# Attention and a gated FFN woven into one instruction stream: the first batch's attention set alone, whole 512-token FFN tiles, even FFN shares, the range count in two parts

## The chip, the cores and the metric

The kernel runs on one core of a Trainium2 chip. The core has a matrix engine (TensorE, PE in the rows), a vector engine (VectorE, DVE), a scalar engine (ScalarE, ACT), a general engine (GpSimd, POOL) and a queue processor (SyncE, SP); 16 DMA engines move data between the device memory (HBM) and the on-chip memory (SBUF), and matmul results go to PSUM, which has eight banks. The metric is the device time of one execution in microseconds; lower is better.

## The reference

Causal attention over 8 batches of 8 heads with 576 positions of 64 numbers, with 16 beacon keys and values ahead of each sequence that every position sees; its output, laid out as 4608 tokens of 512 numbers, goes through a gated feed-forward layer (FFN) of width 1536.

```python
k_all = np.concatenate([beacon_k, k], axis=2)
v_all = np.concatenate([beacon_v, v], axis=2)
scores = scale * np.matmul(q, k_all.transpose(0, 1, 3, 2))
...
scores = np.where(causal, -1000000000.0, scores)
a = np.exp(scores - max)
a /= a.sum(-1, keepdims=True) + 1e-09
x = np.matmul(a, v_all)          # then as 4608 x 512 tokens
...
gate = np.maximum(x @ w_gate, 0.0)
return (gate * (x @ w_val)) @ w_out
```

## The kernel before

The whole program is one list of instructions per engine, written out by a planner in Python; each engine takes its list in order and waits where a buffer or an operand is not ready. Attention for a batch is cut into seven **steps**, and the FFN is cut into nine tiles of 512 tokens. A table `plan` says for each step which batch's attention it holds and how many microseconds of FFN work (the quota) may be put beside it.

**Attention of one step.** A step holds two units. `Unit.qk` writes scores into one of two double-bank PSUM buffers (`s`, L322), `Unit.exp` takes them through the exponential on ScalarE into `e` (L330) and masks the diagonal parts on GpSimd (`affine_select`, L338). When the last unit of a chunk (240, 256 or 80 positions of four heads) has gone, the next step computes `Chunk.av`: the products with the values into `ab` and the row sums into `os` (L364), both in PSUM with one buffer each. `invert` takes the reciprocal of the row sums on VectorE (`r`, L372), `scale` multiplies it into `xT`, the FFN's input (L377), and `report` sends one copy of `r` per head to `rsum` through SP (L384). For batches 0 and 1 the units run chunk by chunk through both groups of four heads (`UNITS_BY_CHUNK`), for the others group by group.

**FFN of one tile.** Twelve `up` groups and four `down` groups. An `up` group is four matmuls into `g` with the gate's weights (L399), a Relu on ScalarE (L402), four matmuls into `u` with the other weights (L405), and the product on VectorE into `hT` (L407). `g` and `u` take turns in the two buffers of the PSUM pool `f_ps`, so the next `g` waits for the Relu and the next `u` for the product. A `down` group is twelve matmuls (L412), a copy on ScalarE (L415) and a store by SP (L417). Tiles 0 and 1 are cut in two pieces each, (0, 240), (240, 512), (512, 816), (816, 1024), so that a piece can start as soon as a chunk of the batch is there; the others are whole. Each step hands groups from `queue` to the lists as long as its credit lasts.

**Loading.** Batches 0 and 1 load k and q in halves (`load_half`, L256, tile `wide`), cast them (`hwide`, L263) and turn them with transposing matmuls through `f_ps` (L274); their 64 last rows go through `turn_rows` (L291, the tails). v is loaded by rows (L226, `raw`) and cast (L241). Batches 2 to 7 are fetched one batch ahead: loads on SP, casts on GpSimd into the pool `half`, and DMA transposes on SP (L250). The weights come in by casting DMAs that GpSimd issues (L298, L303).

**The end.** After step 58 the rest of the queue is emitted in a plain loop. At its fifth group `count_in_range` checks on VectorE that all row sums lie in a range (three operations on `rsum`, a 1-column matmul, L433, and a cast) and loads the count into a register of every engine; after the loop a branch on it skips or runs a general path, which the inputs here don't need.

Of the kernel before, what the change touches and what calls it, by code (L numbers as in the profile page):

```python
# [153 lines left out]
def kernel(  # L154
# [12 lines left out]
    nc = tc.nc  # L167
# [30 lines left out]
    stage = main.enter_context(tc.tile_pool(name="stage", bufs=8))  # L198
    half = main.enter_context(tc.tile_pool(name="half", bufs=6))
    psb = main.enter_context(tc.tile_pool(name="psb", bufs=10))  # L200
    nrm = main.enter_context(tc.tile_pool(name="nrm", bufs=2))
    fsb = main.enter_context(tc.tile_pool(name="fsb", bufs=2))
# [5 lines left out]
    class Batch:  # L208
# [50 lines left out]
        def cast_half(self, x, i, cast):  # L259
            raw = self.raw.pop((x, i, "half")).rearrange("p (h r d) -> p r h d", r=2, d=D)  # L260
            h = self.h[x, i, "half"] = wide.tile([P, 2, d_model], BF16, name="hwide", bufs=2)
            for r in range(2):
                cast(h[:, r].rearrange("p (h d) -> p h d", d=D), raw[:, r])  # L263
# [79 lines left out]
    class Chunk:  # L343
# [6 lines left out]
        def av(self):  # L350
            self.ab = o_ps.tile([P, 2, 256], FP32, name="ab")
            self.os = o_ps.tile([P, 256], FP32, name="os")
            cq0, _, segs = CHUNKS[self.ci]
            order = sorted(segs, key=lambda x: x[0])
            for i, (kt, q0, n, _, _) in enumerate(order):
                e = self.batch.e.pop((self.g, self.ci, kt))
                kr = min(P, Stot - kt * P)
                for part in range(3):
                    for hh in range(4):
                        rows = slice(hh * C, (hh + 1) * C)  # L360
                        c0 = (4 * self.g + hh) * D + part * C
                        w = ones[:kr, :] if part == 2 else self.batch.v[:kr, kt, c0:c0 + C]
                        o = self.os[rows] if part == 2 else self.ab[rows, part]
                        nc.tensor.matmul(  # L364
                            o[:, q0 - cq0:q0 - cq0 + n], w, e[:kr, 2 * (hh % 2) + hh // 2],
                            start=(i == 0 and part != 1), stop=(i == self.last),
                            skip_group_check=True)
# [55 lines left out]

    def count_in_range():
        rows = B * H
        ge = const.tile([rows, S], FP32, name="ge")
        nc.vector.tensor_scalar(out=ge, in0=rsum, scalar1=1e-10, scalar2=None, op0=ALU.is_ge)
        nc.vector.scalar_tensor_tensor(out=ge, in0=rsum, scalar=1e10, in1=ge,
                                       op0=ALU.is_le, op1=ALU.mult)
        ok = const.tile([rows, 1], BF16, name="ok")  # L430
        nc.vector.tensor_reduce(ok, ge, op=ALU.min, axis=AX.X)
        cnt_ps = o_ps.tile([1, 1], FP32, name="os")
        nc.tensor.matmul(cnt_ps, ok, ones[:rows, :1], start=True, stop=True)  # L433
        cnt = const.tile([1, 1], mybir.dt.int32, name="cnt")
        nc.vector.tensor_copy(cnt, cnt_ps)
        return nc.values_load(cnt, min_val=0, max_val=rows,
                              skip_runtime_bounds_check_because="a count of rows")

# [5 lines left out]

    plan = ([(0, i, 4.5 if i > 4 else 0.0) for i in range(STEPS)]
            + [(None, 0, 4.5)] * ALONE
            + [(1, i, 4.0) for i in range(STEPS)]
            + [(b, i, 4.5) for b in range(2, B) for i in range(STEPS)]
            + [(None, 0, 4.5)])

    with tc.manual_schedule():
# [10 lines left out]
        def load_first(x):  # L462
            x.beacon = x.load_rows(beacon_k[x.b])
            x.load_half("k", 0)
            x.load_half("q", 0)
            x.load("v", 0)
            x.load("v", 1)

        def load_rest(x):
            x.load_half("k", 1)  # L470
            x.load_half("q", 1)
            x.load("v", 2)
            x.load("v", 3)
            x.tail_k = x.load_rows(k[x.b, :, 512:])
            x.tail_q = x.load_rows(q[x.b, :, 512:])
            x.load("v", 4)
# [7 lines left out]
        first.cast_half("q", 0, act)  # L484
        first.turn_half("q", 0, (act, dve))
        first.cast("v", 0, pool)
        first.cast("v", 1, pool)

# [4 lines left out]
        def turn_two(x, i, cast):  # L493
            for n in "kq":
                x.cast_half(n, i, cast)
                x.turn_half(n, i, (dve, act))
# [7 lines left out]
        at(0, lambda: turn_two(first, 1, dve))  # L504
        at(0, lambda: load_both(384, 768))
        at(1, lambda: None)
        at(1, lambda: load_both(768, 1536))
        at(2, lambda: first.cast("v", 2, pool))
        at(2, lambda: first.cast("v", 3, pool))
        at(3, lambda: turn_tails(first))  # L510
        at(4, lambda: batches.update({1: Batch(1)}))
# [17 lines left out]
        at(second - 1, lambda: turn_two(batches[1], 1, pool))  # L529
        at(second - 1, lambda: batches[1].cast("v", 1, pool))  # L530
        at(second + 1, lambda: batches[1].cast("v", 2, pool))
        at(second + 1, lambda: batches[1].cast("v", 3, pool))
        at(second + 2, lambda: turn_tails(batches[1]))
        at(second + 3, lambda: batches[1].cast("v", 4, pool))
        at(second + 3, wide_ctx.close)
# [10 lines left out]
        for b in range(2, B):  # L546
            fetch(b, BASE[b] - STEPS)

        spans = ([(0, 240), (240, 512), (512, 816), (816, 1024)]
                 + [(m, m + M_TILE) for m in range(2 * M_TILE, n_tokens, M_TILE)])  # L550
        queue, have, credit = [], 0, 0.0
        due, ready = [], {}

        def run_sp():
            for act_ in later_sp[:]:
                act_()
            later_sp.clear()

        for s, (b, i, quota) in enumerate(plan):
# [9 lines left out]
            if b is not None:  # L569
                if i == 0:  # L570
                    batches[b].e = {}
                order = UNITS_BY_CHUNK if b < 2 else UNITS_BY_GROUP
                units = [Unit(batches[b], order[2 * i + x]) for x in range(2)]
# [19 lines left out]
            for j, (kind, _, run) in enumerate(mine):  # L593
# [3 lines left out]
                if j == 0:  # L597
                    for c in chunks:
                        c.scale()
                        later_sp.append(c.report)  # L600
                if other:
                    other.pop().exp()
            if not mine:
                for c in chunks:
                    c.scale()
                    later_sp.append(c.report)
                if other:
# [3 lines left out]
            for u in units:  # L611
                for g, ci, _, _ in u.parts:
                    left = [x for un in (order[2 * i + 2:]) for x in un if x[:2] == (g, ci)]
                    if not left and not any(c.g == g and c.ci == ci for c in due):
                        due.append(Chunk(batches[b], g, ci))
                        done = [x for un in order[2 * i + 2:] for x in un if x[1] == ci]
                        if not done:
                            ready[s + 2] = b * S + CHUNKS[ci][0] + CHUNKS[ci][1]
        run_sp()
        for t0, _ in spans:  # L620
            queue += ffn_tiles[t0 // M_TILE].groups(0, M_TILE, 0, M_TILE // P)
        for j, (_, _, run) in enumerate(queue):
            if j == 4:
                in_range = count_in_range()
            run()
            run_sp()
    main.close()
    with tc.If(in_range < B * H):
# [31 lines left out]
```

## Time and profile before

| | us |
|---|---|
| median of three runs (lowest, highest) | 445.34 (443.91, 446.67) |
| the profiled execution | 445.8 |
| its span, first to last instruction | 444.1 |
| TensorE busy | 391.2 (88%) |
| ScalarE, VectorE, GpSimd busy | 195.2, 180.6, 123.5 |
| mean granted TensorE clock | 0.963 |

The span is what the rows add up to; the profiled execution's own time is 1.7 us more. "Busy" is the time in which an engine worked on at least one instruction. The granted clock is a share of TensorE's full speed: 1.00 is 2.4 GHz, 0.50 is 1.2 GHz.

### The profile page before, as it was taken

The numbers are of one execution on the slowest core, as the hardware profiler recorded it, in microseconds if no ns is written. First come the engines' busy times: TensorE is split into PE (matmuls) and PEld (weight loads), VectorE is DVE, ScalarE is ACT, GpSimd is POOL, SyncE is SP. The second block draws the span as 40 slices with busy tenths as digits, with TensorE's granted clock in tenths as the row PEclk, the third lists the DMA queues.
The fourth block names the chain that finished last, engine by engine and source line by source line (L and its number), as shares of the span: only waits on it lengthen the run. The fifth ranks groups of instructions, "written<-read, shape, count | busy, mean of one in ns | idle before, by whom it ended". The sixth has DMA issues, their size and how long they took to land.

```text
span 444.1 us, 10502 instructions
## 1 busy us (share of the span) xinstructions
PE 391.2 (88%) x4346; PEld 208.0 (47%) x4393; DVE 180.6 (41%) x256; ACT 195.2 (44%) x290; POOL 123.5 (28%) x220
## 2 busy tenths in 40 slices
PE   3658797799998399999999999999999999699994
PEld 2336565356754244454445444545544554244441
DVE  3544432434433334545543543455345443321320
ACT  3543234454556235446554554564546443123321
POOL 3850511732233415414251434142510200000000
PEclk9999889999999579999999999999999999799998
DMA  8999920794429767637943774458410010001002
GB/s 226 225 224 264 163 54 1 162 206 95 110 71 204 144 150 121 139 104 174 185 108 101 167 174 124 130 131 181 124 40 0 3 73 24 3 23 71 1 25 76
DMA packets 146902, 51.07 MB, mean 115 GB/s; under 512 B 129312, under 2 KB 142240, under 8 KB 146848
## 3 DMA queue, kind: packets, MB, share of 16 engines
q1 hardware_dynamic: 142016, 45.62, 43.9%
q0 software_dynamic: 4832, 4.72, 6.7%
q8 instruction: 36, 0.59, 0.5%
q14 instruction: 18, 0.15, 0.1%
HBM read 38.27 MB, written 9.44 MB: 107 GB/s over the span
## 4 chain that ended last, share of the span: by engine, by line
PE 77%; DVE 7%; issue 4%; POOL 3%; ACT 3%; DMA 2%; SPq 1%; DVEq 0%; ACTq 0%; POOLq 0%
PE f L405 24%; PE f L412 19%; PE f L399 19%; PE ab L364 6%; PE s L322 5%; DVE hT L407 3%; PE os L364 3%; ACT e L330 2%; POOL e L338 1%; DVE r L372 1%; DMA wide<-in_k_dram 1%; PE f L274 1%; DMA rsum<-r 1%; ACT g L402 1%; SPq L226 1%
## 5 line engine op out<-in xcount | busy, mean ns | idle before, releaser
L407 DVE TENSOR_TENSOR hT<-g,f 128x512 bf16<-128x512 f32 (+4 forms) x132 | 77.7, 589 | 142.8 <-PE f L405 132.1
L405 PE MATMUL f<-xT,wv 128*128 128x512 bf16 (+4 forms) x527 | 117.8, 346 | 6.0 <-DVE hT L407 2.7
L330 ACT ACTIVATE e<-s 128x1024 bf16<-128x1024 f32 (+2 forms) x112 | 105.0, 965 | 35.9 <-PE s L322 35.8
L399 PE MATMUL f<-xT,wg 128*128 128x512 bf16 (+4 forms) x502 | 117.0, 349 | 3.6 <-issue 0.9
L402 ACT ACTIVATE g<-f 128x512 f32<-128x512 f32 (+4 forms) x132 | 68.7, 520 | 116.0 <-PE f L399 111.2
L338 POOL TENSOR_SCALAR_AFFINE_SELECT e<-e 128x512 bf16<-128x512 bf16 (+2 forms) x80 | 46.7, 595 | 208.1 <-ACT e L330 197.7
L372 DVE RECIPROCAL r<-os 128x240 f32<-128x240 f32 (+2 forms) x48 | 65.2, 1358 | 89.9 <-PE os L364 83.8
L412 PE MATMUL f<-wo,hT 128*128 128x512 bf16 x412 | 95.2, 379 | 1.5 <-issue 0.6
L405 PEld LDWEIGHTS <-wv 128*128 128x128 bf16 x528 | 51.9, 99 | 62.9 <-issue 27.3
L399 PEld LDWEIGHTS <-wg 128*128 128x128 bf16 x528 | 49.7, 100 | 45.8 <-issue 7.6
L412 PEld LDWEIGHTS <-hT 128*128 128x128 bf16 x432 | 40.9, 98 | 48.7 <-issue 0.4
L364 PE MATMUL ab<-e,v 128*32 128x80 bf16 (+4 forms) x1408 | 44.4, 242 | 10.7 <-DVE xT L377 10.7
L415 ACT COPY ob<-f 128x512 f32<-128x512 f32 x36 | 21.1, 585 | 74.5 <-PE f L412 50.0
L245 POOL CAST half<-raw 128x512 bf16<-128x512 f32 (+2 forms) x60 | 35.4, 612 | 15.0 <-DMA raw<-in_k_dram 10.9
L322 PE MATMUL s<-qT,kT 64*128 64x80 bf16 (+3 forms) x704 | 36.8, 240 | 2.2 <-ACT e L330 1.5
L364 PEld LDWEIGHTS <-v 128*32 128x32 bf16 (+1 forms) x1408 | 27.7, 101 | 20.5 <-DVE xT L377 9.9
L364 PE MATMUL os<-e,ones 128*32 128x80 bf16 (+4 forms) x704 | 35.9, 240 | 0.0
L322 PEld LDWEIGHTS <-kT 64*128 64x128 bf16 x704 | 21.8, 99 | 23.8 <-issue 22.1
L241 POOL CAST v<-raw 128x512 bf16<-128x512 f32 (+1 forms) x40 | 25.5, 640 | 10.4 <-DMA raw<-in_v_dram 10.3
L377 DVE TENSOR_TENSOR xT<-ab,r 128x480 bf16<-128x480 f32 (+2 forms) x48 | 26.6, 553 | 0.7
L364 PEld LDWEIGHTS <-ones 128*32 128x32 bf16 (+1 forms) x704 | 19.9, 103 | 0.5
L274 PE MATMUL f<-ident,hwide 128*128 128x128 bf16 x64 | 8.6, 276 | 10.1 <-DVE hwide L263 3.7
(32 smaller groups left out, 49.5 us busy)
## 6 DMA issues: line engine op xcount, KB each, us to landing
out_dram<-ob SPq DMA_DIRECT2D x36, 256.0 KB
raw<-in_v_dram SPq DMA_DIRECT2D x24, 256.0 KB
raw<-in_q_dram SPq DMA_DIRECT2D x24, 256.0 KB
raw<-in_k_dram SPq DMA_DIRECT2D x18, 256.0 KB
wide<-in_k_dram SPq DMA_DIRECT2D x4, 512.0 KB
wide<-in_q_dram SPq DMA_DIRECT2D x4, 512.0 KB
raw<-in_v_dram SPq DMA_DIRECT2D x8, 224.0 KB
wo<-in_moe_w_out_dram POOLq DMA_DIRECT2D x2, 768.0 KB, 9.5
```

Source lines behind the costliest of these rows:

```text
L245: copy(h[:n], raw[:n])
L322: nc.tensor.matmul(self.s[:, a, c + j * n:c + (j + 1) * n], self.batch.kT[rows, 2 * g + j, kt * P:(kt + 1) * P], self.batch.qT[rows, 2 * g ...
L330: nc.scalar.activation(e[:, :k * 4 * n].rearrange("p (k a x) -> p a k x", k=k, a=2), self.s[:, :, :k * 2 * n].rearrange("p a (k x) -> p a ...
L338: nc.gpsimd.affine_select(out=cols[:, :, :m], in_=cols[:, :, :m], pattern=[[0, 4], [1, m]], compare_op=ALU.is_ge, fill=0.0, base=base, cha ...
L364: nc.tensor.matmul(o[:, q0 - cq0:q0 - cq0 + n], w, e[:kr, 2 * (hh % 2) + hh // 2], start=(i == 0 and part != 1), stop=(i == self.last), sk ...
L372: nc.vector.reciprocal(self.r[:, :n], self.os[:, :n])
L377: nc.vector.tensor_mul(xT[:, 2 * self.g:2 * self.g + 2, t0:t0 + n], self.ab[:, :, :n], self.r[:, :n].unsqueeze(1).to_broadcast([P, 2, n]))
L399: nc.tensor.matmul(g[:, :n], wg[:, ki, nf * P:(nf + 1) * P], x[:, ki], start=(ki == 0), stop=(ki == KM - 1))
L402: nc.scalar.activation(gs[:, :n], g[:, :n], AF.Relu)
L405: nc.tensor.matmul(u[:, :n], wv[:, ki, nf * P:(nf + 1) * P], x[:, ki], start=(ki == 0), stop=(ki == KM - 1))
L407: nc.vector.tensor_mul(self.h[:, nf, c0:c1], gs[:, :n], u[:, :n])
L412: nc.tensor.matmul(o, self.h[:, nf, ms * P:(ms + 1) * P], wo[:, nf, :], start=(nf == 0), stop=(nf == NF - 1))
```

## The change

Six edits are made together.

- **First batch alone.** Steps 0 to 6 (batch 0) get a quota of 0: no FFN group stands in them or in step 7. Its chunks of the second group of heads take their two value banks from `f_ps`, which is free there, so that two chunks can be in work at once. `nrm` has four buffers for `r` instead of two.
- **Whole tiles.** `spans` holds nine spans of 512 tokens; the pieces are gone.
- **Shares.** Batch 1's steps have a quota of 3.2 instead of 4.0, the later ones 4.4 instead of 4.5. Batch 1 runs group by group.
- **Loads.** The second halves of k and q are loaded ahead of v, their k half is cast ahead of step 0 (`hwide` has three buffers, `half` five instead of six), and casts of v, weight loads and tails are put at other steps.
- **Reports.** A report stays back until the next one is there, so SP issues each about one step later.
- **Range count.** The three VectorE operations stay at the fifth group of the last loop, the matmul and the cast come at the eleventh, and the register is loaded after the loop.

```diff
     stage = main.enter_context(tc.tile_pool(name="stage", bufs=8))
-    half = main.enter_context(tc.tile_pool(name="half", bufs=6))
+    half = main.enter_context(tc.tile_pool(name="half", bufs=5))
     psb = main.enter_context(tc.tile_pool(name="psb", bufs=10))
-    nrm = main.enter_context(tc.tile_pool(name="nrm", bufs=2))
+    nrm = main.enter_context(tc.tile_pool(name="nrm", bufs=4))
     fsb = main.enter_context(tc.tile_pool(name="fsb", bufs=2))
...
             raw = self.raw.pop((x, i, "half")).rearrange("p (h r d) -> p r h d", r=2, d=D)
-            h = self.h[x, i, "half"] = wide.tile([P, 2, d_model], BF16, name="hwide", bufs=2)
+            h = self.h[x, i, "half"] = wide.tile([P, 2, d_model], BF16, name="hwide", bufs=3)
             for r in range(2):
...
         def av(self):
-            self.ab = o_ps.tile([P, 2, 256], FP32, name="ab")
-            self.os = o_ps.tile([P, 256], FP32, name="os")
+            spare = self.batch.b == 0 and self.g == 1
+            self.ab = (f_ps if spare else o_ps).tile(
+                [P, 2, 256], FP32, name="f" if spare else "ab")
+            self.os = (f_ps if spare else o_ps).tile([P, 256], FP32, name="f" if spare else "os")
             cq0, _, segs = CHUNKS[self.ci]
...
-    def count_in_range():
+    def rows_in_range():
         rows = B * H
...
         nc.vector.tensor_reduce(ok, ge, op=ALU.min, axis=AX.X)
+        return ok
+
+    def count_rows(ok):
+        rows = B * H
         cnt_ps = o_ps.tile([1, 1], FP32, name="os")
...
         nc.vector.tensor_copy(cnt, cnt_ps)
-        return nc.values_load(cnt, min_val=0, max_val=rows,
-                              skip_runtime_bounds_check_because="a count of rows")
+        return cnt
...
-    plan = ([(0, i, 4.5 if i > 4 else 0.0) for i in range(STEPS)]
+    plan = ([(0, i, 0.0) for i in range(STEPS)]
             + [(None, 0, 4.5)] * ALONE
-            + [(1, i, 4.0) for i in range(STEPS)]
-            + [(b, i, 4.5) for b in range(2, B) for i in range(STEPS)]
+            + [(1, i, 3.2) for i in range(STEPS)]
+            + [(b, i, 4.4) for b in range(2, B) for i in range(STEPS)]
             + [(None, 0, 4.5)])
...
             x.load_half("q", 0)
+            x.load_half("k", 1)
+            x.load_half("q", 1)
+
+        def load_rest(x):
             x.load("v", 0)
             x.load("v", 1)
-
-        def load_rest(x):
-            x.load_half("k", 1)
-            x.load_half("q", 1)
             x.load("v", 2)
...
         first.turn_half("q", 0, (act, dve))
+        first.cast_half("k", 1, dve)
         first.cast("v", 0, pool)
-        first.cast("v", 1, pool)
...
             for n in "kq":
-                x.cast_half(n, i, cast)
+                if (n, i, "half") in x.raw:
+                    x.cast_half(n, i, cast)
                 x.turn_half(n, i, (dve, act))
...
         at(0, lambda: turn_two(first, 1, dve))
-        at(0, lambda: load_both(384, 768))
+        at(0, lambda: first.cast("v", 1, pool))
         at(1, lambda: None)
-        at(1, lambda: load_both(768, 1536))
+        at(1, lambda: load_both(384, 768))
+        at(2, lambda: None)
         at(2, lambda: first.cast("v", 2, pool))
         at(2, lambda: first.cast("v", 3, pool))
+        at(2, lambda: load_both(768, 1536))
+        at(3, lambda: None)
         at(3, lambda: turn_tails(first))
...
         at(second - 1, lambda: turn_two(batches[1], 1, pool))
-        at(second - 1, lambda: batches[1].cast("v", 1, pool))
-        at(second + 1, lambda: batches[1].cast("v", 2, pool))
-        at(second + 1, lambda: batches[1].cast("v", 3, pool))
-        at(second + 2, lambda: turn_tails(batches[1]))
-        at(second + 3, lambda: batches[1].cast("v", 4, pool))
+        at(second - 2, lambda: batches[1].cast("v", 1, pool))
+        at(second, lambda: batches[1].cast("v", 2, pool))
+        at(second, lambda: batches[1].cast("v", 3, pool))
+        at(second + 1, lambda: turn_tails(batches[1]))
+        at(second + 1, lambda: batches[1].cast("v", 4, pool))
         at(second + 3, wide_ctx.close)
...
-        spans = ([(0, 240), (240, 512), (512, 816), (816, 1024)]
-                 + [(m, m + M_TILE) for m in range(2 * M_TILE, n_tokens, M_TILE)])
+        spans = [(m, m + M_TILE) for m in range(0, n_tokens, M_TILE)]
         queue, have, credit = [], 0, 0.0
...
+        reports = []
+
         def run_sp():
-            for act_ in later_sp[:]:
+            for act_ in later_sp:
                 act_()
             later_sp.clear()
+            while len(reports) > 1:
+                reports.pop(0)()
...
                     batches[b].e = {}
-                order = UNITS_BY_CHUNK if b < 2 else UNITS_BY_GROUP
+                order = UNITS_BY_CHUNK if b == 0 else UNITS_BY_GROUP
                 units = [Unit(batches[b], order[2 * i + x]) for x in range(2)]
...
                         c.scale()
-                        later_sp.append(c.report)
+                        reports.append(c.report)
                 if other:
...
                     c.scale()
-                    later_sp.append(c.report)
+                    reports.append(c.report)
                 if other:
...
         run_sp()
+        for report in reports:
+            report()
         for t0, _ in spans:
...
             if j == 4:
-                in_range = count_in_range()
+                ok = rows_in_range()
+            if j == 10:
+                cnt = count_rows(ok)
             run()
             run_sp()
+        in_range = nc.values_load(cnt, min_val=0, max_val=B * H,
+                                  skip_runtime_bounds_check_because="a count of rows")
     main.close()
...
```

What the order of instructions shows (line numbers of each kernel's own file; those of the changed kernel are 2 higher from L374 on).

GpSimd from the first cast of v on: `v` casts, weight loads (`wg`, `wv`), masks of `e`, the tails (`half`). Before:

```order
L241 CAST v<-raw 128x512 x2
L298 DMA wg<-in_moe_w_gate_dram 128x2x384 x2
L298 DMA wv<-in_moe_w_val_dram 128x2x384 x2
L338 AFFINE_SELECT e<-e 128x4x112
L338 AFFINE_SELECT e<-e 128x512 x2
L298 DMA wg<-in_moe_w_gate_dram 128x2x384 x2
L298 DMA wv<-in_moe_w_val_dram 128x2x384 x2
L338 AFFINE_SELECT e<-e 128x4x112
L338 AFFINE_SELECT e<-e 128x512 x2
L298 DMA wg<-in_moe_w_gate_dram 128x2x768 x2
L298 DMA wv<-in_moe_w_val_dram 128x2x768 x2
L338 AFFINE_SELECT e<-e 128x4x128
```

The same place of the changed kernel:

```order
L241 CAST v<-raw 128x512
L298 DMA wg<-in_moe_w_gate_dram 128x2x384 x2
L298 DMA wv<-in_moe_w_val_dram 128x2x384 x2
L338 AFFINE_SELECT e<-e 128x4x112
L338 AFFINE_SELECT e<-e 128x512 x2
L241 CAST v<-raw 128x512
L338 AFFINE_SELECT e<-e 128x4x112
L338 AFFINE_SELECT e<-e 128x512 x2
L298 DMA wg<-in_moe_w_gate_dram 128x2x384 x2
L298 DMA wv<-in_moe_w_val_dram 128x2x384 x2
L338 AFFINE_SELECT e<-e 128x4x128
L241 CAST v<-raw 128x512 x2
```

The second weight loads moved behind the masks of step 1, and the third ones behind the casts of v that follow.

VectorE from the first 256-wide chunk of batch 0 on: `r` and `xT` are a chunk's two operations, each `hT` is one FFN `up` group, the casts and copies turn batch 1. Before:

```order
L372 RECIPROCAL r<-os 128x256
L377 TENSOR_TENSOR xT<-ab,r 128x2x256
L372 RECIPROCAL r<-os 128x256
L407 TENSOR_TENSOR hT<-g,f 128x240
L377 TENSOR_TENSOR xT<-ab,r 128x2x256
L407 TENSOR_TENSOR hT<-g,f 128x240 x5
L372 RECIPROCAL r<-os 128x80
L407 TENSOR_TENSOR hT<-g,f 128x240
L377 TENSOR_TENSOR xT<-ab,r 128x2x80
L407 TENSOR_TENSOR hT<-g,f 128x240 x4
L372 RECIPROCAL r<-os 128x80
L407 TENSOR_TENSOR hT<-g,f 128x240
```

The changed kernel, from the same reciprocal on:

```order
L374 RECIPROCAL r<-os 128x256
L379 TENSOR_TENSOR xT<-ab,r 128x2x256
L374 RECIPROCAL r<-f 128x256
L379 TENSOR_TENSOR xT<-f,r 128x2x256
L374 RECIPROCAL r<-os 128x80
L379 TENSOR_TENSOR xT<-ab,r 128x2x80
L374 RECIPROCAL r<-f 128x80
L288 CAST half<-raw 16x512
L292 COPY kT<-f 128x4x16
L275 COPY kT<-f 128x2x256
L275 COPY qT<-f 128x2x256
L379 TENSOR_TENSOR xT<-f,r 128x2x80
```

All twelve 240-wide products left this place; every second chunk reads `f` where it read `os` and `ab`.

VectorE in the attention of batch 2, with the last products of tile 1 ahead of it in the kernel before:

```order
L407 TENSOR_TENSOR hT<-g,f 128x208
L377 TENSOR_TENSOR xT<-ab,r 128x2x240
L372 RECIPROCAL r<-os 128x256
L377 TENSOR_TENSOR xT<-ab,r 128x2x256
L372 RECIPROCAL r<-os 128x80
L377 TENSOR_TENSOR xT<-ab,r 128x2x80
L372 RECIPROCAL r<-os 128x240
L377 TENSOR_TENSOR xT<-ab,r 128x2x240
L372 RECIPROCAL r<-os 128x256
L377 TENSOR_TENSOR xT<-ab,r 128x2x256
L372 RECIPROCAL r<-os 128x80
L407 TENSOR_TENSOR hT<-g,f 128x512
```

The changed kernel, from batch 2's first reciprocal on:

```order
L374 RECIPROCAL r<-os 128x240
L409 TENSOR_TENSOR hT<-g,f 128x512
L379 TENSOR_TENSOR xT<-ab,r 128x2x240
L409 TENSOR_TENSOR hT<-g,f 128x512 x4
L374 RECIPROCAL r<-os 128x256
L409 TENSOR_TENSOR hT<-g,f 128x512
L379 TENSOR_TENSOR xT<-ab,r 128x2x256
L409 TENSOR_TENSOR hT<-g,f 128x512 x2
L374 RECIPROCAL r<-os 128x80
L409 TENSOR_TENSOR hT<-g,f 128x512
L379 TENSOR_TENSOR xT<-ab,r 128x2x80
L409 TENSOR_TENSOR hT<-g,f 128x512 x2
```

Before, the plan had no `up` group left between batch 2's first chunk and its last one (steps 18 to 22; 20 to 22 held no FFN work at all); now tile 1's twelve whole groups stand there.

## Rows read from the trace of the kernel before

**Rows 1.** The page: the chain that ended last, shares by engine.

```profile
PE 77%; DVE 7%; issue 4%; POOL 3%; ACT 3%; DMA 2%; SPq 1%; DVEq 0%; ACTq 0%; POOLq 0%
```

**Rows 2.** Stretches: us, each engine's busy time (instructions), granted clock, DMA share, GB/s.

```profile
0.00:34.65 34.65, 18.04 (x256) 11.15 (x256) 15.20 (x22) 14.73 (x17) 19.23 (x36) 1.00 1.10 229
70.36:116.59 46.23, 40.51 (x500) 25.39 (x502) 18.51 (x30) 22.37 (x38) 17.48 (x31) 1.00 0.58 124
116.59:157.38 40.79, 30.37 (x535) 19.59 (x539) 14.79 (x22) 18.17 (x27) 15.58 (x28) 0.85 0.64 131
199.60:241.08 41.48, 40.75 (x492) 20.39 (x500) 19.38 (x24) 21.94 (x30) 14.54 (x26) 1.00 0.63 143
...
55.00:60.00 5.00, 5.00 (x26) 3.30 (x25) 0.88 (x2) 1.68 (x4) 1.75 (x3) 0.55 0.65 144
145.00:150.00 5.00, 0.00 (x0) 0.00 (x0) 1.57 (x1) 0.83 (x2) 1.83 (x3) 0.50 1.01 163
160.00:165.00 5.00, 5.00 (x22) 1.94 (x22) 1.62 (x4) 1.60 (x3) 1.22 (x2) 0.81 0.99 224
```

**Rows 3.** The chain in order of time (start, us, what): two tiles' first down groups.

```profile
186.17 2.59 PE f L412 x12
227.65 2.59 PE f L412 x12
```

**Rows 4.** Timeline (start, us, engine, [idle before <-releaser]): one group each of five widths, one down.

```profile
47.70 0.41 DVE L407 TENSOR_TENSOR hT<-g,f 128x240 bf16<-128x240 f32 x1 [0.73 <-PE f L405]
62.67 0.44 DVE L407 TENSOR_TENSOR hT<-g,f 128x272 bf16<-128x272 f32 x1 [0.78 <-PE f L405]
108.91 0.47 DVE L407 TENSOR_TENSOR hT<-g,f 128x304 bf16<-128x304 f32 x1 [0.84 <-PE f L405]
114.67 0.37 DVE L407 TENSOR_TENSOR hT<-g,f 128x208 bf16<-128x208 f32 x1 [0.68 <-PE f L405]
377.37 0.69 DVE L407 TENSOR_TENSOR hT<-g,f 128x512 bf16<-128x512 f32 x1 [1.18 <-PE f L405]
438.07 0.58 ACT L415 COPY ob<-f 128x512 f32<-128x512 f32 x1 [2.05 <-PE f L412]
```

**Rows 5.** Timeline of the stretch in batch 2 with no FFN work.

```profile
148.43 1.66 DVE L372 RECIPROCAL r<-os 128x240 f32<-128x240 f32 x1 [6.11 <-DMA rsum<-r]
150.83 0.62 PE L364 MATMUL ab<-e,v 128*32 128x256 bf16 x8 [6.09 <-DVE xT L377]
```

**Rows 6.** Timeline around the range count.

```profile
378.97 1.03 PE L399 MATMUL f<-xT,wg 128*128 128x512 bf16 x4
381.72 0.44 DVE L427 TENSOR_SCALAR ge<-rsum 64x576 f32<-64x576 f32 x1
383.78 0.16 PE L433 MATMUL os<-ones,ok 64*1 64x1 bf16 x1 [2.77 <-DVE ok L431]
392.90 1.03 PE L399 MATMUL f<-xT,wg 128*128 128x512 bf16 x4
```

**Rows 7.** Timeline of the start.

```profile
26.64 0.39 PE L291 MATMUL f<-ident,half 64*128 64x64 bf16 x4 [2.90 <-POOL half L288]
28.37 0.62 PE L364 MATMUL ab<-e,v 128*32 128x256 bf16 x8
33.39 0.40 PE L364 MATMUL ab<-e,v 128*32 128x256 bf16 x8 [1.81 <-DVE xT L377]
42.50 0.97 ACT L330 ACTIVATE e<-s 128x960 bf16<-128x960 f32 x1 [0.68 <-PE s L322]
51.43 0.25 PE L291 MATMUL f<-ident,half 16*128 16x16 bf16 x4 [1.13 <-DVE half L288]
54.97 1.11 PE L399 MATMUL f<-xT,wg 128*128 128x272 bf16 x4
67.29 0.39 PE L274 MATMUL f<-ident,hwide 128*128 128x128 bf16 x4
70.36 0.60 PE L322 MATMUL s<-qT,kT 64*128 64x240 bf16 x12
```

## The prediction

> **What bounds the kernel now.** I read the chain that ended last first: 77% of it is TensorE and 4% is issue, no other engine has more than 7% [rows 1]. So the time is TensorE's work plus the stretches in which TensorE waits or runs at its low clock, and the stretches say where these are [rows 2]. Between 199.60 and 241.08 TensorE is busy 40.75 of 41.48 us at full clock: nothing is to be had there. Up to 34.65 it is busy 18.04 us, and between 116.59 and 157.38 only 30.37 of 40.79 us, at a mean clock of 0.85; the 5 us from 145 on hold no matmul at all and the clock stands at 0.50, that is 1.2 GHz. The change works on these places and on the range count near the end.
>
> **Prices.** An FFN group's period is read on VectorE as its product plus the idle time before it [rows 4]: 0.69 + 1.18 = 1.87 us for a whole `up` group, 1.14 for 240 columns, 1.22 for 272, 1.31 for 304, 1.05 for 208. A `down` group takes 0.58 + 2.05 = 2.63 us. A whole tile is 12 x 1.87 + 4 x 2.63 = 33.0 us. The first `down` groups of two tiles in a row start 41.48 us apart [rows 3], and with one tile and one batch in that time a batch's attention costs TensorE 8.5 us.
>
> **The change part by part**, as a sum against the span of 444.1 us.
>
> *Whole tiles.* Column for column, 240 of 512 would be 0.88 us of the 1.87, 272 are 0.99, 304 are 1.11 and 208 are 0.76. The pieces take 0.26, 0.23, 0.20 and 0.29 us more each, since the two `f_ps` buffers come round sooner than Relu and product are done. Twelve of each: 11.8 us, of which 5.2 lie ahead of 70.36 (twelve of 240, nine of 272). These are direct readings; I keep 10 to 12.
>
> *Even shares.* Before, tiles 0 and 1 are eaten up early, and in batch 2 the plan runs dry for steps 20 to 22. There TensorE stands still for 6.09 us, behind a reciprocal that waits 6.11 us for a report of `r` to leave its buffer [rows 5]. From batch 2's first scores (116.59) to tile 2's first group (157.38) stand eight groups of 208 (8.4 us), four `down` groups (10.5), and the attention of batch 2 and of one step more (9.7): 28.6 us of work in 40.8. So 12.2 us are lost, and as the clock is still low until about 162 (mean 0.81 from 160 to 165 [rows 2]), 4.5 us at half speed lose 2.2 more. The changed plan has FFN groups in each of these steps, and four buffers for `r` take the wait's cause away: 14.4 us, bounds 11 (batch 2's loads still cost something) and 15.
>
> *Range count.* Four periods from the group at 378.97 to the one at 392.90 should be 7.5 us and are 13.9 [rows 6]: 6.4 us, for TensorE waits in order for the 1-column matmul at 383.78 and for the register load, then runs at the low clock. Split, the matmul comes ten microseconds after its operand. What comes back: the three VectorE operations (381.72 to 383.7, 2.0 us) fit but for 0.8 us into an idle gap of 1.18, and that delay hits a `u` whose turn is one `g` (0.86 us) later, so it hides; the register load at the end lies beside the last store, 438.07 to 444.1 holding a 0.58 us copy and a 256 KB store. I take 5.7 us, bounds 4.5 and 6.4.
>
> *First batch alone.* I compare the moment at which batch 1's first scores are issued, less whole-tile work done by then. Before it is 70.36 [rows 7], with twelve pieces of 240 and nine of 272 done, 10.4 whole groups or 19.5 us; without the pieces' 5.2 us that leaves 45.7 us.
>
> Afterwards I walk it. GpSimd paces the start: TensorE turns the tails at 26.64, after 2.90 us of waiting for their cast [rows 7], and GpSimd's queue up to there holds the same weight loads, masks and casts after the change, in another order. But v now arrives behind a further megabyte of k and q: at the 229 GB/s of this stretch about 4 us, of which the earlier scores give some back. I put the tails at 29. Step 4's products began 1.7 us behind them (28.37) and, four blocks of eight with their row sums at 0.62 us a block, take 2.4: step 5's scores start at 33. The second bank pair removes the 1.81 us wait at 33.39: products until 36.3, step 6's scores until 37, its exponentials (0.97 at 42.50, the narrower second one less) and mask until some 39.1, products until 39.8. Turning batch 1's first halves took from 50.3 (51.43 less a wait of 1.13) to 54.97 and takes it again: 44.5. Three whole groups (5.6 us), the first 4.5 us at the low clock as from 54.97 on (0.55 from 55 to 60 [rows 2]) and so 2.2 us longer, end at 52.3; the second turning, 67.2 to 70.36, ends at 55.5. Less 5.6 us of work that is 49.9: **4.2 us lost**.
>
> The bounds: 49.7 for the early end if GpSimd does not pace it (70.36 less the pieces' 24.7 and their 2.1 at the low clock, plus 7.8 for the three groups, less 1.81 for the second bank pair), that is 5.8 us better; 6 us worse, as long as the longest wait for a transfer in these rows (6.11 us [rows 5]), if batch 1's halves, whose loads now overlap all weight loads (DMA share 1.10 [rows 2]), land late. The second bank pair itself is worth little while GpSimd sets the pace.
>
> On the clock the start shows this: eight products with 256 columns take 0.62 us at 28.37 and 0.40 at 33.39 [rows 7], so TensorE worked at the low level until about 31, though the stretch's granted clock is given as 1.00 (no change is on record before). The Trainium skill ("TensorE: Matmul & The Clock Gate", Part 1) says that the throttled state is the default and that activity releases it, which speaks against a stretch with attention only; the trace agrees in the two durations. By that rule the products of steps 5 and 6 stay at 0.62 for 0.40, some 1.3 us, which the walk, made from the slow durations, already holds.
>
> *Batch 1's steps.* Steps 9 to 15 hold 22 us of FFN and 8.5 of attention, 4.4 us each; before they took 46.2 us, 6.6 each, with 42.6 of work in them (twelve pieces of 304, three of 272, four of 208, four `down` groups, one batch), so 3.6 us of waits. I take the same waits. `half` with five buffers and the later reports cost nothing: a cast needs a buffer whose transpose is more than a step old.
>
> *Sum.* 444.1 - 11.8 - 14.4 - 5.7 + 4.2 = 416.4. Counted directly: 49.9 + nine tiles (297) + seven batches (59.5) + 3.6 + 0.7 of the count + the 6.0 us after the last matmul = 416.7. The profiled execution is 1.7 us over its span and 0.5 over the median: **418 us**, 6% below 445.34. A measurement of this kernel tells about 1% from no change.
>
> **The rivals.**
>
> *The loads set batch 1's pace.* Batch 2's rows, casts and transposes must go by in 31 us instead of 46, while `wo` still arrives. GpSimd takes them in order and stands still for a late row, and the masks behind it hold back the products. For it: a DMA share of 1.10 at the start and 0.58 over those 46 us, which is 0.86 in 31. Against it: steady steps of 5.9 us at a share of 0.63 lose nothing. At worst the steps stay 6.6 us long: seven times 2.2 less the 3.6 of waits already counted, 12 us more, 430.
>
> *A quicker start.* GpSimd's queue holds less ahead of step 1 and does not pace it: 5.8 us less, 412. Against it stands the tails' wait of 2.90 us for GpSimd at 26.64.
>
> *The clock stays low.* Place: steps 8 to 15. If the thinner mixture of short score and product matmuls with one to three FFN groups left TensorE at 1.2 GHz, 36 us of work would take 72: 454, slower than before. It decides from 27 us of work at the low level on. The same page of the Trainium skill ("Why this matters for your kernels") warns of gaps between bursts. Against it: the low stretches at 55 and at 157 ended after some 4.5 us of back-to-back FFN groups, and steps 9 to 15 ran at 1.00 throughout [rows 2].
>
> *The wait only moves.* The even shares leave batch 2 short of something else (its fetch starts at step 9 either way), the 14.4 us come back and the start loses 6 to 10: 438 to 442, hardly to be told from no change.
>
> **How the numbers follow.** My forecast within 6 us has a chance of 0.60, the loads' pace 0.18, the quicker start 0.15, the clock 0.03, the moved wait 0.04. The likeliest is 418. The range takes in the quicker start with the better bounds of the sum (410) and most of the loads' case (429). Faster by over 1% needs less than 440.9: 0.94; within 1%: 0.03; slower: 0.03.
>
> **What the changed profile would show.** Batch 1's first scores at 52 to 59 us; no `up` group narrower than 512; `up` periods of 1.87 us from there on; no stretch of 5 us without a matmul and full clock in batch 2; steps of 4.4 us in batch 1, 41 us per later batch; no gap over 1 us at the range count; the last matmul about 6 us ahead of the end. The prediction is wrong if GpSimd waits for rows in batch 1 or if the clock falls again after the first FFN groups.

## The result, and the profile after

The changed kernel took 425.81 us (423.03 to 429.41) against 444.75 us (443.91 to 446.67): a ratio of 0.9548, 95% interval 0.9485 to 0.9610. A second set of runs gave 422.27 us (420.0 to 427.98), ratio 0.9486 (0.9443 to 0.9529). Both profiled executions of it (429.41 and 427.98 us) were the longest of their sets, count as slow and are left out of the ratios. The forecast of 418.0 us had the sign and most of the size and was 4 to 8 us too low.

The chain that ended last, on the page of the changed kernel (span 427.7 us):

```profile
PE 81%; ACT 0%; DVE 0%; issue 0%; POOL 0%; ACTq 0%; DVEq 0%
```

This chain is followed back only to 72.57 us, so it says nothing of the start; from there on it is TensorE's work almost alone, where DVE had 7% and issue 4% of a chain that began at 2.37 us [rows 1]. Stretches of the changed kernel (columns as in [rows 2]):

```profile
30.00:40.00 10.00, 6.63 (x252) 5.09 (x243) 5.78 (x6) 4.20 (x6) 4.60 (x8) 0.82 1.15 237
40.00:45.00 5.00, 0.00 (x0) 0.00 (x0) 0.00 (x0) 0.00 (x0) 0.28 (x1) 0.55 1.22 217
45.00:50.00 5.00, 0.85 (x8) 0.71 (x9) 1.67 (x4) 0.00 (x0) 0.00 (x0) 0.50 1.22 199
...
63.98:99.64 35.66, 33.82 (x398) 16.30 (x397) 17.00 (x21) 19.07 (x25) 17.50 (x31) 0.90 0.56 121
99.64:141.11 41.47, 41.47 (x497) 20.38 (x497) 19.37 (x24) 21.94 (x30) 14.77 (x26) 1.00 0.65 143
```

The last two rows are batch 1's steps (first scores to batch 2's first scores) and batch 2's. Batch 2 has lost its hole: 41.47 us, all busy, at full clock, where before 30.37 of 40.79 were busy [rows 2]. The second and third show what the forecast lacked: between batch 0's end and batch 1's turning TensorE stands still, at 1.2 GHz, while the DMA share is at its highest (1.22; the share adds up the time of all packets, so it can pass 1). The timeline there (start, us, what, [idle before <-releaser]):

```profile
27.26 6.54 SPq L256 DMA_DIRECT2D wide<-in_q_dram  x1
27.72 0.39 PE L291 MATMUL f<-ident,half 64*128 64x64 bf16 x4 [7.29 <-POOL half L288]
33.90 4.47 SPq L386 DMA_DIRECT2D rsum<-r  x1
47.29 0.66 DVE L374 RECIPROCAL r<-f 128x80 f32<-128x80 f32 x1 [9.41 <-DMA rsum<-r]
48.27 0.27 PE L291 MATMUL f<-ident,half 16*128 16x16 bf16 x4 [9.55 <-DVE half L288]
52.13 0.63 POOL L241 CAST v<-raw 128x512 bf16<-128x512 f32 x1 [11.85 <-DMA raw<-in_v_dram]
53.19 1.91 PE L401 MATMUL f<-xT,wg 128*128 128x512 bf16 x4
63.98 0.69 PE L322 MATMUL s<-qT,kT 64*128 64x240 bf16 x12
```

Up to 37 us the walk held, its times a microsecond or two too late: the tails at 27.7 (forecast 29), 0.36 us of waiting for value banks. Then the sixth reciprocal of batch 0, which takes the second chunk's buffer of `r`, waits for that chunk's report. SyncE, held in the loads of batch 1's halves, issued it only at 33.90. The beacon cast and all of batch 1's turning stand behind it on VectorE. Batch 1's first scores come at 63.98 us (before: 70.36 [rows 7]; forecast: 55.5). Less the three groups done by then that is 58.4 us, against 45.7 before by the prediction's own measure.

The range count now:

```profile
362.36 0.69 DVE L409 TENSOR_TENSOR hT<-g,f 128x512 bf16<-128x512 f32 x1 [1.18 <-PE f L407]
...
365.67 1.02 PE L407 MATMUL f<-xT,wv 128*128 128x512 bf16 x4 [0.69 <-ACT g L404]
...
374.11 0.16 PE L439 MATMUL os<-ones,ok 64*1 64x1 bf16 x1
```

One wait of 0.69 us is left of the stall of [rows 6], and the period of a whole group is the 1.87 us of [rows 4].

### The profile page after: what moved, and what is told of

Read it like the earlier page. It is cut to its first block, busy times and chain, and to the rows that moved or that the text cites. A ratio compares the mean times of both kernels' runs of the same rounds, so it can differ in the third digit from the quotient of the medians.

```text
span 427.7 us, 10075 instructions
## 1 busy us (share of the span) xinstructions
PE 385.5 (90%) x4201; PEld 188.3 (44%) x4201; DVE 175.8 (41%) x232; ACT 191.9 (45%) x266; POOL 124.0 (29%) x220
## 4 chain that ended last, share of the span: by engine, by line
PE 81%; ACT 0%; DVE 0%; issue 0%; POOL 0%; ACTq 0%; DVEq 0%
PE f L407 23%; PE f L414 22%; PE f L401 22%; PE s L322 6%; PE ab L366 6%; PE os L366 2%; DVE hT L409 0%; ACT g L404 0%; ACT ob L417 0%; POOL half L288 0%; PE f L291 0%; PE os L439 0%; ACTq L417 0%; DVEq L409 0%
## 5 line engine op out<-in xcount | busy, mean ns | idle before, releaser
L409 DVE TENSOR_TENSOR hT<-g,f 128x512 bf16<-128x512 f32 x108 | 74.2, 687 | 123.2 <-PE f L407 116.6
L401 PE MATMUL f<-xT,wg 128*128 128x512 bf16 x432 | 114.1, 388 | 0.0
L407 PE MATMUL f<-xT,wv 128*128 128x512 bf16 x432 | 112.8, 384 | 1.0 <-ACT g L404 0.7
L404 ACT ACTIVATE g<-f 128x512 f32<-128x512 f32 x108 | 64.5, 597 | 90.6 <-PE f L401 90.6
L374 DVE RECIPROCAL r<-os 128x240 f32<-128x240 f32 (+2 forms) x45 | 61.1, 1357 | 83.9 <-PE os L366 83.9
L407 PEld LDWEIGHTS <-wv 128*128 128x128 bf16 x432 | 42.3, 98 | 63.8 <-issue 21.8
L401 PEld LDWEIGHTS <-wg 128*128 128x128 bf16 x432 | 40.0, 99 | 47.3 <-issue 3.4
L366 PE MATMUL ab<-e,v 128*32 128x80 bf16 (+4 forms) x1320 | 40.0, 236 | 0.0
L366 PE MATMUL os<-e,ones 128*32 128x240 bf16 (+3 forms) x660 | 32.4, 234 | 0.0
L291 PE MATMUL f<-ident,half 64*128 64x64 bf16 (+1 forms) x24 | 1.9, 201 | 22.1 <-DVE half L288 12.8
```

Of the source, the lines that this page charges most:

```text
L366: nc.tensor.matmul(o[:, q0 - cq0:q0 - cq0 + n], w, e[:kr, 2 * (hh % 2) + hh // 2], start=(i == 0 and part != 1), stop=(i == self.last), sk ...
L374: nc.vector.reciprocal(self.r[:, :n], self.os[:, :n])
L401: nc.tensor.matmul(g[:, :n], wg[:, ki, nf * P:(nf + 1) * P], x[:, ki], start=(ki == 0), stop=(ki == KM - 1))
L404: nc.scalar.activation(gs[:, :n], g[:, :n], AF.Relu)
L407: nc.tensor.matmul(u[:, :n], wv[:, ki, nf * P:(nf + 1) * P], x[:, ki], start=(ki == 0), stop=(ki == KM - 1))
L409: nc.vector.tensor_mul(self.h[:, nf, c0:c1], gs[:, :n], u[:, :n])
```

## The experiments

The ratios are all to the kernel before in the same set of runs, about 444.5 us. The first theory: the 9.4 us wait for the report is the miss. Its rival: the loads bind, and something else takes the wait's place.

**Own buffers for the 80-column reciprocals** (424.19 us, ratio 0.9552, 0.9483 to 0.9621).

```
-self.r = nrm.tile([P, 256], FP32, name="r")
+self.r = (nrm.tile([P, 256], FP32, name="r") if n > 80
+          else nrm.tile([P, 80], FP32, name="rt", bufs=2))
```

> The changed kernel, but the 80-column reciprocals get two buffers of their own, so that none of batch 0's six waits for a report. Theory (the sixth reciprocal stood 9.4 us on VectorE for the report of the second chunk, and batch 1's turning behind it): the first turning starts at 38 to 39 us instead of 48.3, three groups follow, and the second turning then waits for GpSimd's casts of the second halves, which stand behind the v casts of batch 1 (52.1 us); batch 1's first scores near 58 instead of 64.0, 420 us. Rival (loads: batch 1's rows arrive too late whatever the reciprocal does, DMA share 1.2 there): another wait, ended by a load, takes its place and the time stays within 2 us of 425.8.

Its timeline:

```profile
40.68 0.27 PE L291 MATMUL f<-ident,half 16*128 16x16 bf16 x4 [1.02 <-DVE half L288]
...
52.05 0.65 POOL L241 CAST v<-raw 128x512 bf16<-128x512 f32 x1 [11.92 <-DMA raw<-in_v_dram]
54.11 0.28 PE L274 MATMUL f<-ident,hwide 128*128 128x128 bf16 x2 [1.13 <-POOL hwide L263]
57.64 1.01 PE L322 MATMUL s<-qT,kT 64*128 64x240 bf16 x12
```

The trace does what the theory says (turning at 40.7, then GpSimd behind v, first scores at 57.6, span 421.1 instead of 427.7), but the median is no better than the changed kernel's. From batch 2's first scores to the end the profiles of the changed kernel and of these first four runs all take 328.0 to 328.1 us. If the other runs do too, the three of the changed kernel's first set, with spans of 421.2 to 424.4, had those scores at 93.2 to 96.4 and, less the 35.6 us of batch 1's steps, batch 1's first scores at 57.6 to 60.8; the six of its second set (418.1 to 421.3) had these at 54.5 to 57.7. Worked out so, the long wait is in the profiled executions and at most a part of it in these.

**Reports at once** (423.76 us, 0.9538, 0.9469 to 0.9607): `while len(reports) > 1` becomes `while reports`.

> The changed kernel with every report issued one step after its chunk, none held back: the second chunk's report goes out ahead of batch 1's loads on SyncE. Four buffers of r as in the changed kernel. Theory (place in SyncE's order): the sixth reciprocal finds its buffer free, the same 420 us as with buffers of its own, or up to 2 us more where SyncE later waits for a chunk's scaling. Rival (the report is late because the DMA engines are full, not because of its place): it lands some 10 us after issue again, and the time stays within 2 us of 425.8.

The sixth reciprocal ran at 39.5 us without a wait for a report, the turning began at 41.2, the first scores came at 58.5: the place in SyncE's order is what makes the wait possible. The median again does not move.

**Own buffers, and v cast last** (423.51 us, 0.9511, 0.9424 to 0.9599). Batch 1's first two v casts go behind the second halves' casts; with this the second turning also stands ahead of the three groups.

```
-at(second - 2, lambda: batches[1].cast("v", 0, pool))
 at(second - 1, lambda: turn_two(batches[1], 1, pool))
-at(second - 2, lambda: batches[1].cast("v", 1, pool))
+at(second - 1, lambda: batches[1].cast("v", 0, pool))
+at(second - 1, lambda: batches[1].cast("v", 1, pool))
```

> As with buffers of their own, and on GpSimd the casts of batch 1's second halves stand ahead of its first two v casts. Theory: nothing is left that holds the second turning, batch 1's first scores at 53 to 56 us (the prediction's walk said 55.5), 416 to 418 us. Rival (loads): the halves themselves land late and the time stays at 424 to 426; or the v casts, now later, hold the first products of batch 1, and the gain over the kernel with own buffers is gone within 1 us.

GpSimd's casts of the second halves, in its timeline:

```profile
46.44 1.17 POOL L263 CAST hwide<-wide 128x512 bf16<-128x512 f32 x2 [4.69 <-DMA wide<-in_k_dram]
...
52.55 1.17 POOL L263 CAST hwide<-wide 128x512 bf16<-128x512 f32 x2 [4.94 <-DMA wide<-in_q_dram]
```

The rival's numbers: the second halves themselves land late, q at 52.5 us. Batch 1's first scores come at 62.9, now behind the three groups; batch 2's at 95.9. The four runs fall into two pairs, near 421 and near 426 us, and the profile is of the slower pair.

**One bank pair** (423.12 us, 0.951, 0.9438 to 0.9582): `spare = False`.

> The changed kernel without the second pair of value banks: all chunks of batch 0 use o_ps. Theory (GpSimd's casts pace the start and the report of the second chunk ends it): the products of the second group wait some 2 us each at 32 and 36 us, the sixth reciprocal still waits until 47, no change, within 1 us of 425.8. Rival (the bank pairs matter): three waits of 1.8 us, 430 to 431 us.

No change, as the theory said, but not for its reason. The products of the second group do wait (1.81, 1.85 and 1.24 us), the sixth reciprocal runs at 42.80 instead of 39.7 as with own buffers, and by then the report has landed: it waits 1.42 us, for its matmul. First scores at 58.2. In none of these four profiles do they come before 57.6. In three of them GpSimd casts the second halves behind v, which lands at 52 to 54 us, and in the one with v last the second q half itself lands at 52.5: what they share is a late load. That the loads are the cause is tried next.

**The changed kernel again** (422.27 us).

> The changed kernel as it is, a second profile. From batch 2's first scores to the end the profiles of the changed kernel and of the four runs before all take 328 us, so a span of 421 to 424 needs these scores at 93 to 96 us. If the 9.4 us wait of the sixth reciprocal is a matter of chance in when a report lands, it is shorter here, the first turning starts at 39 to 44 us, and the second turning waits for GpSimd's cast behind v (52 us). If the wait belongs to the order, it is 9 us again and the span near 427.

The profile shows the wait again, and first scores at 62.30; it was the longest of seven runs.

```profile
45.94 0.66 DVE L374 RECIPROCAL r<-f 128x80 f32<-128x80 f32 x1 [7.64 <-DMA rsum<-r]
```

The wait is in the order in both profiles; how long it is differs (9.41 and 7.64 us).

**wo later** (424.47 us, 0.9529, 0.9482 to 0.9576): own buffers, v cast last (the three groups ahead of the second turning again), and

```
-at(6, lambda: load_wo(0, 6))
-at(6, lambda: load_wo(6, 12))
+at(9, lambda: load_wo(0, 6))
+at(9, lambda: load_wo(6, 12))
```

> Buffers of their own for the 80-column reciprocals, second halves cast ahead of v on GpSimd, the three groups ahead of the second turning, and wo loaded from step 9 on instead of step 6. New theory (the 16 DMA engines are full until some 53 us, share 1.2, and the rows of batch 1 share them with the weights): wo's 1.57 MB, as the profile counts them, are 7 us of the engines at 225 GB/s; without them the second q half, which landed at 52.5 us, lands by 47, and batch 1's first scores come at 55 us: 418 to 419 us. Rival (the loads do not bind, GpSimd's and VectorE's order does): no later than 57.6 us and no gain, 423 to 424 us.

The second q half is cast at 44.66 us instead of 52.55: 7.9 us for wo's 1.57 MB, forecast 7. First scores only 56.50, and batch 2 gives the rest back, as the second line shows at its second score matmuls:

```profile
44.66 1.17 POOL L263 CAST hwide<-wide 128x512 bf16<-128x512 f32 x2 [1.00 <-DMA wide<-in_q_dram]
...
94.19 0.29 PE L322 MATMUL s<-qT,kT 64*128 64x128 bf16 x4 [2.63 <-DMA qT<-half]
```

wo, issued at 58.7, may now stand in the way of batch 2's rows and transposes; the last of these runs tries that.

**Weights later too** (420.17 us, 0.9444, 0.9398 to 0.949): `load_both(768, 1536)` goes from step 2 to step 7, behind `second_first`.

> As with wo late, and the last half of gate and value weights is issued at step 7 instead of step 2. New theory: 1.57 MB less ahead of batch 1's rows, and GpSimd does not issue them ahead of the tails (2.85 us): tails turned at 25 us, batch 1's first scores at 51 to 53 us, 415 to 417 us. Rival (loads do not bind): only the tails come earlier, 421 us. Against both: if the weights now come too late for the groups of step 11 (69 us), a wait for them there, some 5 us, 420 to 424.

Tails at 25.9, first scores at 51.94, as the load theory had it, but TensorE again waits 2.45 us for batch 2's transposes: 420 instead of 415 to 417.

```profile
90.26 0.29 PE L322 MATMUL s<-qT,kT 64*128 64x128 bf16 x4 [2.45 <-DMA qT<-half]
```

**wo in the hole** (417.74 us, 417.01 to 418.36; 0.9401, 0.937 to 0.9432): as the one before, wo at step 8 behind the v casts. The second turning stands ahead of the three groups here, so that order changed together with wo's place.

> As with the weights late, but wo is issued at step 8 (42 us) instead of step 9 (54 us), into the stretch from 50 to 55 us in which the DMA share was 0.52. Theory (with the weights late, what is left is wo in the way of batch 2's rows: TensorE waited 2.45 us at 90 us for a transpose of q): this wait is gone, batch 1's first scores stay at 52, 417.7 us. Rival (the engines have no room before 90 us; each load put off delays the next): the wait stays or batch 1's v comes late, 420 us.

The stretch from 50 to 55 us with the weights late (columns as in [rows 2]):

```profile
50.00:55.00 5.00, 3.97 (x29) 2.27 (x30) 0.69 (x1) 2.21 (x4) 1.40 (x3) 0.66 0.52 117
```

The same stretch with wo in the hole:

```profile
50.00:55.00 5.00, 5.00 (x31) 2.12 (x30) 1.37 (x2) 2.16 (x3) 0.00 (x0) 0.91 1.22 196
```

The DMA share there goes from 0.52 to 1.22: wo is loaded in time that was free, and the wait for batch 2's transposes is gone; batch 1's first scores come at 53.56, batch 2's at 87.65. This version beats both kernels: its interval lies below those of both sets of the changed kernel. The kernel with the same buffers and v cast last, but no load moved, took 423.51 us and never less than 420.9. The six runs here lie within 1.35 us, where the changed kernel's second set spreads over 8; but the four with reports at once lie within 1.2.

The other terms of the sum, one part at a time.

**Pieces put back** into the changed kernel (436.45 us, 0.98, 0.9721 to 0.988): `spans` as before the change.

> The changed kernel with the pieces of 240, 272, 304 and 208 columns for tiles 0 and 1; no step of its plan is empty. The prediction's term by itself: 11.8 us more, 436 us. By the new theory (the start waits for loads): 11 pieces of 240 run where three whole groups ran, in time that TensorE stood idle, so their 2.9 us are hidden and 3.2 us of work are done earlier: 5.7 us more, 430 us. Rival (the pieces' price was slack): no change.

The ratios of this set (0.98 against 0.9486) differ by 14.0 us, some 4 either way by their intervals: the prediction's 11.8 fits, the 5.7 of the load theory doesn't. The extra time of pieces is not hidden in the start's idle time: in its profile batch 1's first scores come at 66.03, batch 2's at 104.58, and the 328.0 us from there on are as before.

**Range count split, alone, in the kernel before** (439.06 us, 0.9875, 0.9842 to 0.9909; the four edits of `count_in_range` and of the last loop in the diff).

> The kernel before with the range count split as in the change (matmul at the eleventh group of the last loop, register load behind the last), and nothing else. The prediction's term by itself: 5.7 us less (4.5 to 6.4), 439.2 us. Rival (the stall is only moved to the end, where the register load is on the path): no change, 444.9 us.

5.6 us (4.0 to 7.0). The trace has waits of 0.20 and 0.69 us left at this place, the changed kernel only the second.

**Four buffers of r, alone, in the kernel before** (444.04 us, 0.9992, 0.9957 to 1.0027): `name="nrm", bufs=4`.

> The kernel before with four buffers of r instead of two, and nothing else. If the reciprocal's 6.11 us wait in batch 2 is what stops TensorE there: 4 to 6 us less, 439 to 441 us. Rival (batch 2 is out of FFN work at steps 20 to 22 and its exponentials and rows set the pace with or without the wait): within 1 us of 444.9, with another wait in the place of this one.

No change. In the place of [rows 5] its timeline has this, a few microseconds on:

```profile
154.74 0.40 PE L322 MATMUL s<-qT,kT 64*128 64x128 bf16 x4 [4.54 <-DMA qT<-half]
```

**Even shares, alone, in the kernel before** (433.04 us, 0.976, 0.9715 to 0.9806).

```
-+ [(1, i, 4.0) for i in range(STEPS)]
-+ [(b, i, 4.5) for b in range(2, B) for i in range(STEPS)]
++ [(1, i, 3.2) for i in range(STEPS)]
++ [(b, i, 4.5 if b > 2 else 3.2) for b in range(2, B) for i in range(STEPS)]
```

> The kernel before with a share of 3.2 us a step in batches 1 and 2, so that no step of these is without an FFN group; pieces, start and the rest as before. The prediction's term by itself: 14.4 us less (11 to 15), 430.5 us. Rival (batch 2 is short of its rows or of buffers of r, and the wait only moves): 3 to 7 us less, 438 to 442.

The edit is not quite the change's: batch 2 has 3.2 here and 4.4 there, and the pieces stay. 10.7 us (8.6 to 12.7) by the ratio: nearer to the term's lower bound of 11 than to 14.4. The profiled execution (span 429.5) shows the full 14.6; the runs fall into two groups, 431 and 435 us, the faster one with the higher mean granted clock (0.986 to 0.990 against 0.967 to 0.982), and what separates them is open.

## Why the prediction was right, and where it was short

*What bounds the kernel, whole tiles, range count, steady part:* right. 11.8 was forecast for the pieces and 14.0 measured, 5.7 for the range count and 5.6 measured. From batch 2's first scores on, the forecast's own numbers leave 416.7 - 55.5 - 34.1 = 327.1 us; the trace has 328.1, with 41.47 us for batch 2 (forecast 41) and no group narrower than 512 columns. The last matmul ends 6.7 us ahead of the end (forecast 6). Two slips in the prediction's sums change nothing: the bound of 49.7 adds up to 49.6, and batch 1's steps stand there at 4.4 us each, but at 4.9 in the sum, which adds the 3.6 us of waits.

*Even shares:* right in place, large in size, 10.7 for 14.4. "Four buffers for `r` take the wait's cause away" named the wrong half of it: alone they are worth nothing, since batch 3's transposes are late next. FFN work in these steps is what fills the hole. Some luck is in the total: 2.2 us too little for the pieces make up for part of the 3.7 too much here.

*First batch alone* is the step that failed: 4.2 us lost was forecast. The changed kernel's ratios (20.1 and 22.9 us) less the three parts measured singly (30.3) leave 7 to 10 us lost; by their intervals this is open by some 4 to 6 us, and parts tried singly need not add up, so this is a size and no more. In the profiled execution, step by step, 8.5 of the miss of 11.0 (span 427.7 for 416.7) lie ahead of batch 1's first scores, 1.6 in batch 1's steps (35.66 us, forecast 34.1, with the low clock again from 64 to 68 and from 75 to 78 us: four gate matmuls take 1.89 us for 1.03), 1.0 behind. In the other runs, as worked out above (first scores at 54.5 to 60.8 for 55.5), the first of these is 5 us at most. The walk priced GpSimd and TensorE only and let the loads in as a bound ("6 us worse ... if batch 1's halves, whose loads now overlap all weight loads, land late"). That bound was the case, in the profiled execution with 2.5 us on top: batch 1's rows, the weights and wo fill the engines to some 50 us (share 1.22), and four orders of VectorE and GpSimd (the first four runs) all stay at 423 to 424 us, while two moved weight loads, with own buffers and the order of the casts, bring 418. "The later reports cost nothing" was wrong too, for a report held back one chunk falls behind batch 1's loads; but it shows only in the executions in which it is the longer of two waits. That report was my first theory for the whole miss. It fell: taking the wait away in two ways left the median where it was.

The prediction named two signs of being wrong, and both came in the profile: GpSimd waits 11.85 us for batch 1's rows of v, and the clock falls again after the first three groups. First scores at 52 to 59 us and steps of 4.4 us in batch 1 did not come either (63.98 and 5.1). So the time lies in the range, but on the side of the loads, not by the likeliest course: the first set's median is 7.8 us over the forecast, outside the 6 us that were given a chance of 0.60, the second set's 4.3.

*The rivals.* The loads' pace had the right cause and the wrong place: not batch 1's steps (35.7 us, far from the 46.2 it named) but the turning ahead of them. The clock did not stay low, though it fell twice more: from 80 us on it is at 1.00 (until TensorE's work ends). The quicker start did not come: TensorE waits 7.29 us for GpSimd at the tails. On the clock of the start, the products with 256 columns take 0.61 to 0.65 us a block of eight up to the one at 33.20 and 0.39 at 33.75, and the granted clock goes from 0.50 (32 to 33 us) to 1.00 (34 to 35): half of step 5's products were slow, step 6's no longer. The rise came earlier than the forecast had it, which kept the products of both steps slow. The Trainium skill ("TensorE: Matmul & The Clock Gate", Part 1) has the rule that activity releases the throttled state; the trace agrees in these durations.

## What to carry to other kernels

Where the DMA share stands above 1, as here up to 50 us, take a walk along the compute queues as a lower bound only: list the loads in the order of their first use, and what each pushes back, before a wait on an engine gets a price. A wait taken away in such a stretch showed in the trace and not in the time; moving a load that nobody needs yet into a stretch with room did both. Ask of every wait what is late next: twice here (the reports, four buffers of `r`) it was a transfer a few microseconds on.

## What the runs showed of the hardware

A 3.8 KB report issued on SyncE at 33.90 us, behind 2 MB of loads, took 4.47 us to issue and held the next writer of its buffer until 47.29; the two 512 KB loads ahead of it held SyncE for 4.78 and 6.54 us, where the two before these took 1.43 and 0.53. wo is issued by GpSimd and yet held back SyncE's loads by 7.9 us. The Trainium skill ("DMA: Bandwidth & Descriptors", section "Issuing engines are not separate DMA queues") says that transfers started by either engine run on the same 16 DMA engines and interleave; the trace agrees in those 7.9 us.
